# A parameter set for a kernel that orders its own work, and a start whose loads are issued by two engines

## The chip, the cores and the metric

One core of a Trainium2 chip runs the program. The metric is the device time of one execution in microseconds (us). Every time below is of this one core. TensorE is called PE in the views (PEld for its weight loads), VectorE is DVE, ScalarE is ACT, GpSimd is POOL, and SyncE, which issues most transfers, is SP.

## What is computed

For 8 batches, 8 heads, 576 positions and 64 features per head, attention keeps the 32 largest scores of a row, and its result goes through a layer that takes the largest of three products:

```python
scores = scale * np.matmul(q, k.transpose(0, 1, 3, 2))
kth = np.partition(scores, -top_k, axis=-1)[..., -top_k:-top_k + 1]
scores = np.where(scores >= kth, scores, -1000000000.0)
attn = softmax(scores)                       # written out in the reference
x = np.matmul(attn, v).transpose(0, 2, 1, 3).reshape(B * S, H * D)
h = np.maximum(np.maximum(x @ w1, x @ w2), x @ w3)     # 512 -> 768
out = h @ w_out                                        # 768 -> 512
```

q, k and v are float32, the four weights are float64.

## The kernel before

Two heads share one pass (a head pair, 4 pairs to a batch). A unit of work is one pair and 256 of its rows, or two pairs and the last 64 rows of each; a batch has 10 units. A unit goes through these steps. PE computes scores (`qk`, L514), ACT copies them out (`evac`, L523), DVE takes the eight largest of each 72 columns (`sweep`, L532) and finds a pivot (L546 to L563). ACT takes the sign against it (L571), POOL multiplies (L576), DVE takes eight maxima again (L580), picks the 32nd largest and masks (L619). ACT takes the exponential (L628), PE transposes it (`turn`, L674 to L679), ACT copies it out (L687), PE multiplies by v (`values`, L704). DVE, ACT and POOL turn the result into two half-precision parts, `xh` and `xl` (L721 to L728).

The layer (`mlp`) of a batch takes its 576 rows in spans of columns. For a span, each of 6 blocks f of 128 hidden features needs three products of 12 matmuls each (`layer`, L760): 216 matmuls for a span. ACT and DVE keep the largest (L767, L769), ACT and POOL split it into `hh` and `hl` (L772, L775). Then `layer2` (L820) makes 128 output rows with 18 matmuls, ACT scales them (L825) and SP stores them (L831 to L835). Batches 0 to 6 have spans of 256 and 320 columns; `parts_of[B - 1]` (L1056) gives the last batch 256, 256 and 64.

The weights arrive as float64 in 18 blocks (`load_weight`, L229, 768 KB each for the first 12). DVE builds float32 of the two words, half a block at a time (`decode`, L238 to L240): the first half of a block reads the first 768 of its 1536 words in a row. ACT squares the result (L250), PE sums the squares (L259). `load_qk` (L420 to L431) issues the six transfers of one head pair: two for q, two for k, and two for the last 64 rows of k and of q (tile `last`). PE transposes `last`, k and q (L454, L465), ACT and POOL make `kT` and `qT` of them (L469 to L474).

No scheduler of the compiler orders this work. Each step is a `Piece` with an engine, a cost in ns, the pieces it needs, the buffers it takes and a rank. `in_order` (L65) plays the pieces through its own model of the five engines and emits them in that order; each engine then runs its own list strictly in order. A piece's rank is the place of its unit plus a number from the table `OFFSETS`. Of the pieces near the lowest rank (`LEAD`, `WINDOW`), an engine takes the first that can start within `PATIENCE` of the earliest. The layer's pieces are a second list (`fill`), which PE takes where it would otherwise wait (`AHEAD_OF_FILL`). `LOCK_A` and `LOCK_B` say how DVE pieces that read two tensors from SBUF and POOL pieces are kept apart. These constants alone decide which engine does what in which order; the arithmetic does not depend on them.

Of the kernel before, what the change touches and what calls it, by code (L numbers as in the profile page):

```python
# [12 lines left out]
I32 = mybir.dt.int32  # L13
# [15 lines left out]
GAP = 100.0  # L29
NEAR = 110.0  # L30
SWITCH = 95.0
AHEAD_OF_FILL = 3
WINDOW = 150
LEAD = 43.3
SLACK = 2000.0
LOCK_A = -150.0
LOCK_B = -100.0
OFFSETS = {'C0': -8.46, 'C1': -18.47, 'C2': 3.93, 'C3': 15.97, 'D0': -3.87, 'D1': -3.6, 'D2': -21.98, 'D3': 12.25, 'E00': 3.88, 'E01': 0.84, 'E02': -2.21, 'E10': -0.98, 'E11': -2.42, 'E12': -13.91, 'N': 0.27, 'Pa': -3.56, 'Pl': -8.36, 'Pp': 14.6, 'Pz': 7.25, 'R': 10.23, 'S': -1.09, 'T00': -15.17, 'T01': -13.99, 'T02': 4.17, 'T10': -11.04, 'T11': -8.12, 'T12': 22.63, 'U': -1.67, 'U0': 2.18, 'V': -13.7, 'V0': -0.21, 'Y': 0.84, 'Z': -6.48, 'd0': 7.84, 'd1': -2.02, 'e00': -1.82, 'e01': -1.45, 'e10': -1.05, 'e11': 1.55, 'g0': 1.61, 'g1': -2.4, 'g2': 1.3, 'g3': -10.18, 'h0': 2.46, 'h1': -2.33, 'h2': 1.34, 'k0': 0.45, 'k1': -2.6, 'k2': 2.19, 'k3': -8.03, 'm0': -18.11, 'm1': -7.69, 'm2': -3.59, 'm3': -1.01, 'p1': 3.73, 'p2': 4.11, 'p3': -13.92, 'p4': -15.96, 'p5': 2.73, 'q0': -0.76, 'q1': -0.22, 'r0': 1.77, 'r1': -17.21, 's00': 5.74, 's01': 5.23, 's10': 5.37, 's11': 6.45, 'v': 13.6, 'w0': 9.7, 'w1': 11.03, 'w2': 0.57, 'w3': 18.45, 'x0': 3.87, 'x1': 2.76, 'x2': 8.01, 'x3': 5.15, 'y': -13.4, 'z0': 3.01, 'z1': 4.39}
AHEAD = 4
LATE = {'PE': 102.0, 'DVE': 60.0, 'ACT': 95.0, 'POOL': 10.0, 'SP': 2000.0}  # L40

# [91 lines left out]
SPLIT = (0,)  # L133
FIRST = ((0, 1),)
NSM = 2
PATIENCE = {'PE': 2.0, 'DVE': 159.0, 'ACT': 47.0, 'POOL': 7.0, 'SP': 0.0}


@with_exitstack
def kernel(ctx, tc, q, k, v, moe_w1, moe_w2, moe_w3, moe_w_out, out):  # L140
    nc = tc.nc
    B, H, S, D = q.shape
    P = 128
# [76 lines left out]
    def load_weight(j):  # L220
        src, c, n, at0 = parts[j]
        if c % 2 == 0:
            raw = wall.bitcast(I32)[:, 2 * CUT + at0:2 * CUT + at0 + 2 * n]
        elif j < 3 * KC:
            spare = N_IN + 2 * CUT + c // 2 * 2 * DF
            raw = wall.bitcast(I32)[:, spare:spare + 2 * n]
        else:
            raw = wk.tile([P, 2 * n], I32, name="ssb", bufs=NSSB)
        nc.sync.dma_start(raw, src[c * P:(c + 1) * P, :].bitcast(I32))  # L229
        raw_of[j] = raw.rearrange("p (n t) -> p n t", t=2)  # L230

    def decode(j, j0):
# [97 lines left out]
    def weights():  # L330

        decoded, loads, scales = {}, {}, {}
        for i in range(4):
            mine = range(i * KC, (i + 1) * KC) if i < 3 else range(3 * KC, len(parts))
            rank = (0.0, f"D{i}")
            done = []
            release = []
            for j in mine:
                n = parts[j][2]

                free, c = [], parts[j][1]
                takes = [("ssb" if i == 3 else "odd", free)] if c % 2 else []
                needs = [decoded[j - AHEAD]] if j >= AHEAD else []
                if i == 3:
                    needs += [decoded[k] for k in range(3 * KC) if k % 2]
                loads[j] = piece("SP", 5000 if i < 3 else 3400, lambda j=j: load_weight(j), needs, (0.0, f"D{i}"), takes)
                for j0 in range(0, n, PIECE[n]):
                    rel = []
                    x = piece("DVE", 1600 if i < 3 else 1950, lambda j=j, j0=j0: decode(j, j0),
                              [loads[j], *([decoded[j - 1]] if j else []), *([x] if j0 else [])], rank, [("ob", rel), ("ob", rel)], alone=True)  # L350
                    rel.append(x)
                decoded[j] = x
                free.append(x)
                rel = []
                y = piece("ACT", 733 if i < 3 else 510, lambda j=j: square_w(j), [x], rank, [("junk", rel)])
                if i < 3:
                    z = piece("PE", 400, lambda j=j: sum_w(j), [y, *done[-1:]], rank, [("m", release)] * 2 if j % KC == 0 else [])
                    z.slack = SLACK / 4
                    rel.append(z)
                    done.append(z)  # L360
                else:
                    rel.append(y)
                    done.append(y)
            if i < 3:
                scaled = piece("DVE", 1750 if i < 2 else 3000, lambda i=i: column_scale(i), done, rank)
# [27 lines left out]
    def main_rows(t, b, h):  # L393
        return t[at.get(b, b), h, 0:MAIN].rearrange("(p c) d -> p c d", c=NU)
# [24 lines left out]

    def load_qk(b, hp):  # L420
        tiles = []
        for src, nm in ((q, "qt"), (k, "kt")):
            t = io.tile([P, NU, 2, D], F32, name=nm, bufs=1)
            for h in range(2):
                nc.sync.dma_start(t[:, :, h, :], main_rows(src, b, 2 * hp + h))
            tiles.append(t)
        t = io.tile([P, 2, D], F32, name="last", bufs=1)
        for w, src in enumerate((k, q)):
            nc.sync.dma_start(t[64 * w:64 * w + 64], src[at.get(b, b), 2 * hp:2 * hp + 2, MAIN:S].rearrange("h p d -> p h d"))
        tiles.append(t)  # L430
        qk_of[b, hp] = tiles  # L431

# [302 lines left out]
    def mlp(b, first, spans, tiles, alone, needs, rank):  # L735
# [41 lines left out]
        for c0, c1 in spans:  # L777
# [3 lines left out]
            for f in range(FC):  # L781
                box, prev, before = {}, None, []
                for i in range(3):
                    rel = []
                    for kcs in ((0, 1), (2, 3)):
                        x = add("PE", 6 * max(0.423 * w, 64.0), lambda i=i, f=f, kcs=kcs, c0=c0, c1=c1, box=box: layer(i, f, kcs, c0, c1, box),
                                [*needs, *(lows[i * KC + kc, f * P // CUT * CUT] for kc in kcs if lows)],
                                [("m", rel)] if kcs[0] == 0 else [])
                    now = []
                    y = add("DVE" if i else "ACT", 117 + 1.047 * w if i else 152 + 0.844 * w, lambda i=i, w=w, box=box: largest(i, w, box),  # L790
                            [x, *prev] if i else [x], [("h1", now)])
                    rel.append(y)
                    if i:
                        before.append(y)
                    before, prev = now, [y]
# [88 lines left out]
    def attention(n):  # L884
# [3 lines left out]
        half = us[0] == NU  # L888
        gs = range(len(us))
        d = of[n] = {}  # L890
        p = lambda key, *a, **kw: d.setdefault(key, piece(*a, rank=(place_of[n], key if isinstance(key, str) else "".join(map(str, key))), **kw))
# [105 lines left out]

    def prepare(pi):
        b, hp = preps[pi]
        rank = starts[pi]  # L1000
        load = piece("SP", 4000, lambda: load_qk(b, hp), list(load_last), (rank, "Pl"))
        box = {}
        load_last.clear()
        done, last = [], list(load_bits)
# [1 line left out]
        for k in range(3):  # L1006
# [5 lines left out]
            x = piece("PE", 109 if k == 0 else 436, products, [load, *done[-1:]], (rank, "Pp"), [("tr", rel)])  # L1012
            y = piece("ACT", 169 if k == 0 else 1211, lambda k=k: box["turns"][k][1](), [x, *last, *done[-1:]], (rank, "Pa"))
            rel.append(y)
            load_last.append(x)
            if pi >= 2:
                users[pi - 2].append(x)
            done.append(y)
            if k:
                z = piece("POOL", 1380, lambda k=k: box["turns"][k][2](), [y], (rank, "Pz"))  # L1020
                done.append(z)
                load_bits.append(z)
        prepared[pi] = done
# [127 lines left out]
```

## Time and profile before

| what | value |
| --- | --- |
| median of 3 runs | 1278.31 us (1277.34 to 1278.84) |
| the profiled execution | 1279.52 us, span 1277.8 us |
| mean granted clock of TensorE | 0.961 |
| PE busy | 1165.9 us (91%) |
| DVE busy | 1157.3 us (91%) |
| ACT busy | 1118.2 us (88%) |
| POOL busy | 684.9 us (54%) |
| moved by DMA | 53.58 MB, mean 42 GB/s |

The span runs from the first to the last instruction; the execution's own time is 1.7 us longer. Busy shares are averages over stages: at the start DVE and the transfers work and PE has little to do, at the end PE works alone. So the table says little by itself, and the prediction reads the views by stretch of time.

### The profile page before, as it was taken

The page shows a single profiled execution, that of the slowest core. Times are in us where ns is not written, and L with a number is a line of the kernel's source. Part 1 is how long each engine was busy: PE and PEld are TensorE (multiplying, and loading weights), DVE is VectorE, ACT ScalarE, POOL GpSimd, SP SyncE. Part 2 cuts the span into 40 slices and gives each one's busy share as a digit, 9 for nine tenths or more (in the row PEclk, how much of TensorE's full clock was granted, in tenths as well). Part 3 has the DMA queues.
Part 4 walks back from the last instruction along what each step waited for, and adds up shares of the span by engine and source line. Part 5 has one row for each costly group of instructions (what it writes and reads, how often), then busy time and mean ns, then how long its engine had stood idle before and what let it go on. Part 6 is the DMA issues. An engine that isn't in the chain of part 4 may idle for free.

```text
span 1277.8 us, 30699 instructions
## 1 busy us (share of the span) xinstructions
PE 1165.9 (91%) x9949; PEld 855.3 (67%) x9949; DVE 1157.3 (91%) x5736; ACT 1118.2 (88%) x2912; POOL 684.9 (54%) x625
## 2 busy tenths in 40 slices
PE   4337897999799999999999999999999999999997
PEld 3224574766487766867686766867787777867775
DVE  6999999999999999999999999999999999999221
ACT  5699989999999999999999999999999999998321
POOL 4538477664565565655465565555556555545110
PEclk9667899899799999999999999999999999999999
DMA  7341110211011012110111011010111100000000
GB/s 223 129 117 45 51 38 17 49 38 46 20 39 41 25 29 54 30 36 25 51 38 37 20 37 47 20 53 22 46 30 46 30 21 26 20 18 2 17 18 28
DMA packets 107018, 53.58 MB, mean 42 GB/s; under 512 B 91745, under 2 KB 99937, under 8 KB 106849
## 3 DMA queue, kind: packets, MB, share of 16 engines
q1 hardware_dynamic: 106848, 51.54, 14.7%
q8 instruction: 80, 1.31, 0.4%
q14 instruction: 90, 0.73, 0.2%
HBM read 42.07 MB, written 9.44 MB: 40 GB/s over the span
## 4 chain that ended last, share of the span: by engine, by line
PE 33%; DVE 26%; ACT 20%; POOL 4%; issue 2%; SPq 0%; DMA 0%; ACTq 0%; DVEq 0%; POOLq 0%
PE m L760 16%; DVE L L532 6%; DVE ssb L619 6%; DVE Q L580 4%; ACT w L571 4%; PE m L820 4%; ACT pm L628 4%; PE tr L704 4%; ACT pT L687 4%; PE tr L679 4%; POOL w L576 3%; PE s L514 3%; ACT ssb L523 3%; DVE h L769 2%; DVE nR L556 1%
## 5 line engine op out<-in xcount | busy, mean ns | idle before, releaser
L576 POOL TENSOR_TENSOR w<-ssb,w 128x576 f32<-128x576 f32 x288 | 413.6, 1454 | 135.2 <-ACT w L571 134.3
L760 PE MATMUL m<-xh,wall 128*128 128x256 f16 (+2 forms) x2448 | 436.9, 279 | 1.3 <-DVE h L769 0.6
L760 PEld LDWEIGHTS <-wall 128*128 128x128 f16 x3672 | 343.8, 98 | 79.7 <-issue 7.4
L760 PE MATMUL m<-xl,wall 128*128 128x256 f16 (+2 forms) x1224 | 335.2, 279 | 0.0
L532 DVE MAX8 L<-ssb 128x8 f32<-128x72 f32 x2304 | 329.7, 219 | 2.2 <-ACT ssb L523 2.2
L619 DVE SCALAR_TENSOR_TENSOR ssb<-ssb,kth 128x576 f32<-128x576 f32 x288 | 240.8, 864 | 2.3
L628 ACT ACTIVATE pm<-ssb,nb 128x576 f32<-128x576 f32 x288 | 225.5, 785 | 18.5 <-DVE ssb L619 18.3
L571 ACT ACTIVATE w<-ssb,Q 128x576 f32<-128x576 f32 x288 | 226.1, 786 | 6.8 <-DVE Q L563 6.8
L687 ACT COPY pT<-tr 128x512 f32<-128x512 f32 (+1 forms) x432 | 217.8, 520 | 11.3 <-PE tr L676 7.9
L580 DVE MAX8 Q<-w 128x8 f32<-128x576 f32 x288 | 213.9, 750 | 9.7 <-POOL w L576 8.3
L679 PE MATMUL tr<-ident,pm 128*128 128x128 f32 x1152 | 183.3, 285 | 28.4 <-ACT pm L628 13.2
L514 PE MATMUL s<-kT,qT 64*128 64x288 f32 x1920 | 179.8, 322 | 23.0 <-ACT ssb L523 14.7
L523 ACT COPY ssb<-s 128x576 f32<-128x576 f32 x288 | 185.0, 646 | 4.2 <-PE s L514 3.8
L679 PEld LDWEIGHTS tr<-ident,pm 128*128 128x128 f32 x1152 | 130.8, 143 | 80.2 <-ACT pm L628 27.3
L704 PE MATMUL tr<-pT,vt 128*64 128x256 f32 (+1 forms) x1920 | 180.9, 340 | 2.3 <-ACT pT L687 2.1
L514 PEld LDWEIGHTS s<-kT,qT 64*128 64x128 f32 x1920 | 140.6, 195 | 62.0 <-issue 23.8
L775 POOL TENSOR_TENSOR hl<-h,hh 128x256 f16<-128x256 f32 (+2 forms) x102 | 78.3, 768 | 180.2 <-ACT hh L772 171.1
L769 DVE SCALAR_TENSOR_TENSOR h<-m,rises,h 128x256 f32<-128x256 f32 (+2 forms) x204 | 100.4, 492 | 60.1 <-PE m L760 55.9
L704 PEld LDWEIGHTS tr<-pT,vt 128*64 128x64 f32 x1920 | 109.5, 141 | 60.9 <-issue 15.8
L820 PE MATMUL m<-wall,hh 128*128 128x512 f16 x432 | 128.9, 379 | 3.6 <-POOL wall L305 1.9
L728 POOL TENSOR_TENSOR xl<-xs,xh 128x256 f16<-128x256 f32 (+1 forms) x80 | 52.4, 655 | 126.6 <-ACT xh L724 126.6
L474 POOL TENSOR_TENSOR kT<-raws,kT 128x576 fp32r<-128x576 f32 x34 | 49.7, 1462 | 86.2 <-ACT kT L470 83.8
(109 smaller groups left out, 1468.2 us busy)
## 6 DMA issues: line engine op xcount, KB each, us to landing
wall<-in_moe_w_dram SPq DMA_DIRECT2D x12, 768.0 KB, 5.9
qt<-in_q_dram SPq DMA_DIRECT2D x68, 128.0 KB, 2.9
kt<-in_k_dram SPq DMA_DIRECT2D x68, 128.0 KB, 3.0
out_dram<-ob SPq DMA_DIRECT2D x32, 256.0 KB, 2.3
vt<-in_v_dram SPq DMA_DIRECT2D x32, 128.0 KB, 2.1
vt<-in_v_dram SPq DMA_DIRECT2D x32, 64.0 KB, 2.2
vt<-in_v_dram SPq DMA_DIRECT2D x96, 16.0 KB, 2.0
vt<-in_v_dram SPq DMA_DIRECT2D x32, 48.0 KB, 2.2
```

The lines of the kernel that those rows point to most:

```text
L514: nc.tensor.matmul(s[:, h, :HALF], qT[sl, qa, c0:c0 + P], kT[sl, ka, i * HALF:(i + 1) * HALF], start=(n_ == 0), stop=(n_ == len(runs) - 1))
L523: nc.scalar.copy(d["both", g][:, :, i * HALF:(i + 1) * HALF], d["s"].pop((g, i))[:, :, :HALF])
L532: nc.vector.max(d["L"][:, t, k, :], d["ssb"][t][:, k * GW:(k + 1) * GW])
L571: nc.scalar.activation(d["w"][t], d["ssb"][t], AF.Sign, bias=d["Q"][:, t, 0:1], scale=-1.0, accum_out=d["cnt"][:, t:t + 1])
L576: nc.gpsimd.tensor_tensor(d["w"][t], d["ssb"][t], d["w"][t], ALU.mult)
L580: nc.vector.max(d["Q"][:, t, 1:NW], d["w"].pop(t))
L619: nc.vector.scalar_tensor_tensor(ss, ss, d["kth"][:, t:t + 1], ss, ALU.is_lt, ALU.subtract, accum_out=d["lost"][:, t:t + 1])
L628: nc.scalar.activation(d["pm", t // 2][:, t % 2], d["ssb"][t], AF.Exp, bias=d["nb"][:, t:t + 1], scale=-1.0 / SHRINK, accum_out=d["sums"][ ...
L679: nc.tensor.transpose(pt[:, j * P:(j + 1) * P], pm[:, i, 64 * i + j * P:64 * i + (j + 1) * P], ident)
L687: nc.scalar.copy(pT[:, 512 * i:512 * i + m] if i < 2 else pT[:, 8 * P:10 * P], pt[:, :m])
L704: nc.tensor.matmul(to, vt[:, block if i < 4 else 8 + h, :], keys, start=(i == 0), stop=(i == 4))
L760: nc.tensor.matmul(box["ps", i][:, :c1 - c0], a, bb[:, kc, c0:c1], start=(kc == 0 and k == 0), stop=(kc == KC - 1 and k == 2))
```

## The change

Three things are altered in the text.

First, for the first head pair alone, `load_qk` has k and both parts of `last` issued by ACT in place of SP, and the first weight block is loaded in two halves of 768 words; with the costs that the planner has for the first loads, the first block comes second on SP.

Second, the last batch's layer has the spans of all other batches, 256 and 320 columns.

Third, the planner's constants are others: `OFFSETS` has keys of its own for batch 0 (with an underscore ahead), and `LEAD`, `PATIENCE`, `AHEAD_OF_FILL`, `LOCK_A`, `LOCK_B` and one cost are changed.

```diff
-AHEAD_OF_FILL = 3
+AHEAD_OF_FILL = 6
-LEAD = 43.3
+LEAD = 103.6
-LOCK_A = -150.0
-LOCK_B = -100.0
-OFFSETS = {'C0': -8.46, 'C1': -18.47, 'C2': 3.93,
+LOCK_A = -144.0
+LOCK_B = -103.0
+OFFSETS = {'C0': -11.16, 'C1': -38.66, 'C2': 8.85,
...
-PATIENCE = {'PE': 2.0, 'DVE': 159.0, 'ACT': 47.0, 'POOL': 7.0, 'SP': 0.0}
+PATIENCE = {'PE': 87.0, 'DVE': 178.0, 'ACT': 43.0, 'POOL': 73.0, 'SP': 0.0}
...
-        nc.sync.dma_start(raw, src[c * P:(c + 1) * P, :].bitcast(I32))
+        for j0 in range(0, 2 * n, n if j == 0 else 2 * n):
+            m = n if j == 0 else 2 * n
+            nc.sync.dma_start(raw[:, j0:j0 + m], src[c * P:(c + 1) * P, :].bitcast(I32)[:, j0:j0 + m])
...
-                loads[j] = piece("SP", 5000 if i < 3 else 3400, lambda j=j: load_weight(j), needs, (0.0, f"D{i}"), takes)
+                loads[j] = piece("SP", (5000 if j else 3700) if i < 3 else 3400, lambda j=j: load_weight(j), needs, (0.0, f"D{i}"), takes)
...
+        other = nc.sync if qk_of or T_of else nc.scalar
...
-                nc.sync.dma_start(t[:, :, h, :], main_rows(src, b, 2 * hp + h))
+                (other if src is k else nc.sync).dma_start(t[:, :, h, :], main_rows(src, b, 2 * hp + h))
...
-            nc.sync.dma_start(t[64 * w:64 * w + 64], src[at.get(b, b), 2 * hp:2 * hp + 2, MAIN:S].rearrange("h p d -> p h d"))
+            other.dma_start(t[64 * w:64 * w + 64], src[at.get(b, b), 2 * hp:2 * hp + 2, MAIN:S].rearrange("h p d -> p h d"))
...
-                        x = add("PE", 6 * max(0.423 * w, 64.0), lambda i=i, f=f, kcs=kcs, c0=c0, c1=c1, box=box: layer(i, f, kcs, c0, c1, box),
+                        x = add("PE", 6 * max(0.423 * w + 0.9, 29.0), lambda i=i, f=f, kcs=kcs, c0=c0, c1=c1, box=box: layer(i, f, kcs, c0, c1, box),
...
-        rank = starts[pi]
-        load = piece("SP", 4000, lambda: load_qk(b, hp), list(load_last), (rank, "Pl"))
+        rank, first_ = starts[pi], "" if b else "_"
+        load = piece("SP", 4000 if pi else 2400, lambda: load_qk(b, hp), list(load_last), (rank, first_ + "Pl"))
...
-    parts_of[B - 1] = [(True, [(0, 2 * P)], (0, 1)), (False, [(2 * P, 4 * P)], (2, 3)), (False, [(4 * P, S)], (NU,))]
```

Two places show the new order. In the lists, the names ahead of an arrow are tiles that are written; the changed file's line numbers are 2 higher in the weight load and 3 higher from `load_qk` on.

The start of SP before, where `wall` is the weights' tile:

```order
L425 DMA qt<-in_q_dram 128x4x64 x2
L425 DMA kt<-in_k_dram 128x4x64 x2
L429 DMA last<-in_k_dram 64x2x64
L429 DMA last<-in_q_dram 64x2x64
L229 DMA wall<-in_moe_w_dram 128x1536 x2
```

The start of SP in the changed kernel:

```order
L428 DMA qt<-in_q_dram 128x4x64 x2
L231 DMA wall<-in_moe_w_dram 128x768 x2
L231 DMA wall<-in_moe_w_dram 128x1536
L428 DMA qt<-in_q_dram 128x4x64 x2
L428 DMA kt<-in_k_dram 128x4x64 x2
```

The start of ACT in the changed kernel:

```order
L428 DMA kt<-in_k_dram 128x4x64 x2
L432 DMA last<-in_k_dram 64x2x64
L432 DMA last<-in_q_dram 64x2x64
L463 ACT_TABLE_LOAD
L463 ACTIVATE raws<-tr 128x2x64
```

The four transfers of k and `last` moved from SP to ACT, ahead of its table load, and the first weight block stands behind q alone.

PE around the last pair of value products of the main program, before (`tr<-pT,vt` is the value product of one head pair, `m<-wall,hh` belongs to `layer2`):

```order
L820 LDWEIGHTS hl
L820 MATMUL m<-wall,hl 128x512
L704 MATMUL tr<-pT,vt_89 64x64 x10
L704 MATMUL tr<-pT,vt_90 64x64 x10
L820 LDWEIGHTS hh
L820 MATMUL m<-wall,hh 128x512
```

The same place in the changed kernel:

```order
L763 LDWEIGHTS wall
L763 MATMUL m<-xl,wall 128x256
L707 MATMUL tr<-pT,vt_89 64x64 x10
L707 MATMUL tr<-pT,vt_90 64x64 x10
L763 LDWEIGHTS wall
L763 MATMUL m<-xh,wall 128x256
```

Before, PE was still in `layer2` of batch 6 when the last attention products came; now it has finished that and is in the first span of batch 7.

## Rows read from the trace of the kernel before

**Rows 1.** Busy time by stretch: us, then per engine busy us (instructions), clock, DMA share, GB/s

```profile
10.00:128.00 118.00, 58.30 (x310) 37.99 (x310) 113.04 (x437) 92.79 (x225) 67.71 (x64) 0.71 0.40 123
128.00:256.00 128.00, 110.52 (x930) 80.46 (x930) 122.98 (x584) 117.69 (x315) 80.19 (x77) 0.95 0.15 40
...
512.00:640.00 128.00, 127.90 (x1112) 95.11 (x1110) 125.43 (x673) 123.46 (x323) 70.83 (x60) 1.00 0.14 35
...
896.00:1024.00 128.00, 127.79 (x1128) 95.15 (x1127) 124.09 (x648) 124.90 (x329) 74.45 (x63) 1.00 0.15 38
```

**Rows 2.** Chain that ended last, from 1150 us on: start us, us, what

```profile
1190.59 1.32 PE tr L704 x40
1191.90 3.34 PE m L820 x15
...
1196.66 22.27 PE m L760 x204
1218.93 7.77 PE m L820 x36
1226.71 23.58 PE m L760 x216
...
1266.99 4.00 PE m L820 x18
```

**Rows 3.** The same chain, a stretch of batch 6's 320-column span

```profile
1168.24 3.26 PE m L760 x24
```

**Rows 4.** Instructions in order of time, PE, first and last rows of the 64-column span

```profile
1257.89 0.22 PE L760 MATMUL m<-xh,wall 128*128 128x64 f16 x2
...
1266.93 0.59 PE L820 MATMUL m<-wall,hh 128*128 128x512 f16 x2
```

**Rows 5.** Instructions in order of time, all engines, the first 22 us

```profile
0.74 1.28 ACT L460 ACT_TABLE_LOAD   x1 [0.74 <-PEq L1135]
0.74 1.38 SPq L425 DMA_DIRECT2D qt<-in_q_dram  x2
...
2.16 1.30 SPq L425 DMA_DIRECT2D kt<-in_k_dram  x2
...
3.51 0.64 SPq L429 DMA_DIRECT2D last<-in_k_dram  x1
4.19 0.61 SPq L429 DMA_DIRECT2D last<-in_q_dram  x1
4.85 1.07 SPq L229 DMA_DIRECT2D wall<-in_moe_w_dram  x2
...
7.00 0.44 PE L454 MATMUL tr<-ident,last 128*128 128x128 f32 x1 [7.00 <-DMA last<-in_q_dram]
...
7.48 0.28 ACT L460 ACTIVATE raws<-tr 128x128 f32<-128x128 f32 x1 [5.46 <-PE tr L454]
...
9.63 0.36 DVE L238 TENSOR_SCALAR ob<-wall 128x384 int32<-128x384 int32 x1 [8.15 <-DMA wall<-in_moe_w_dram]
...
17.62 4.40 DVE L532 MAX8 L<-ssb 128x8 f32<-128x72 f32 x32
```

**Rows 6.** Busy time by stretch, one us at the start (columns of rows 1)

```profile
2.00:3.00 1.00, 0.00 (x0) 0.00 (x0) 0.00 (x0) 0.02 (x1) 0.81 (x6) 1.00 0.55 126
...
4.00:5.00 1.00, 0.00 (x0) 0.00 (x0) 0.00 (x0) 0.00 (x0) 0.00 (x0) 1.00 0.97 220
```

**Rows 7.** Who waited for whom, DVE, 10 to 1150 us: total us, times, longest

```profile
DVE Q L580 <- POOL w L576: 8.3, 18, 0.9
DVE xs L721 <- PE tr L704: 3.0, 4, 1.8
```

**Rows 8.** Groups of DVE in the first 256 us: busy us, mean ns

```profile
L619 DVE SCALAR_TENSOR_TENSOR ssb<-ssb,kth 128x576 f32<-128x576 f32 x43 | 40.5, 962 | 0.3
...
L239 DVE SCALAR_TENSOR_TENSOR ob<-wall,ob 128x384 int32<-128x384 int32 x24 | 18.1, 754 | 0.8
L240 DVE SCALAR_TENSOR_TENSOR wall<-wall,ob 128x384 int32<-128x384 int32 x24 | 17.1, 714 | 0.8
```

**Rows 9.** One line's instructions: ns min/median/max, L619 to 256 us, L240 to 130

```profile
L619 DVE SCALAR_TENSOR_TENSOR ssb<-ssb,kth x43: 793/814/1949, 63.5 to 253.9; 128x576 f32<-128x576 f32 x43
...
L240 DVE SCALAR_TENSOR_TENSOR wall<-wall,ob x25: 557/559/1641, 11.7 to 117.9; 128x384 int32<-128x384 int32 x24, 128x512 int32<-128x512 int32 x1
```

More of the change, by code (lines that the diff above doesn't have):

```diff
@@ L31 @@
 SWITCH = 95.0
-AHEAD_OF_FILL = 3
+AHEAD_OF_FILL = 6
 WINDOW = 150
-LEAD = 43.3
+LEAD = 103.6
 SLACK = 2000.0
-LOCK_A = -150.0
-LOCK_B = -100.0
-OFFSETS = {'C0': -8.46, 'C1': -18.47, 'C2': 3.93, 'C3': 15.97, 'D0': -3.87, 'D1': -3.6, 'D2': -21.98, 'D3': 12.25, 'E00': 3.88, 'E01': 0.84, 'E02': -2.21, 'E10': -0.98, 'E11': -2.42, 'E12': -13.91, 'N': 0.27, 'Pa': -3.56, 'Pl': -8.36, 'Pp': 14.6, 'Pz': 7.25, 'R': 10.23, 'S': -1.09, 'T00': -15.17, 'T01': -13.99, 'T02': 4.17, 'T10': -11.04, 'T11': -8.12, 'T12': 22.63, 'U': -1.67, 'U0': 2.18, 'V': -13.7, 'V0': -0.21, 'Y': 0.84, 'Z': -6.48, 'd0': 7.84, 'd1': -2.02, 'e00': -1.82, 'e01': -1.45, 'e10': -1.05, 'e11': 1.55, 'g0': 1.61, 'g1': -2.4, 'g2': 1.3, 'g3': -10.18, 'h0': 2.46, 'h1': -2.33, 'h2': 1.34, 'k0': 0.45, 'k1': -2.6, 'k2': 2.19, 'k3': -8.03, 'm0': -18.11, 'm1': -7.69, 'm2': -3.59, 'm3': -1.01, 'p1': 3.73, 'p2': 4.11, 'p3': -13.92, 'p4': -15.96, 'p5': 2.73, 'q0': -0.76, 'q1': -0.22, 'r0': 1.77, 'r1': -17.21, 's00': 5.74, 's01': 5.23, 's10': 5.37, 's11': 6.45, 'v': 13.6, 'w0': 9.7, 'w1': 11.03, 'w2': 0.57, 'w3': 18.45, 'x0': 3.87, 'x1': 2.76, 'x2': 8.01, 'x3': 5.15, 'y': -13.4, 'z0': 3.01, 'z1': 4.39}
+LOCK_A = -144.0
@@ new lines @@
+LOCK_B = -103.0
+OFFSETS = {'C0': -11.16, 'C1': -38.66, 'C2': 8.85, 'C3': 15.4, 'D0': -9.99, 'D1': -8.22, 'D2': -81.18, 'D3': 12.51, 'E00': 4.08, 'E01': -2.19, 'E02': -3.0, 'E10': -1.33, 'E11': -0.86, 'E12': -0.76, 'N': 2.46, 'Pa': -2.78, 'Pl': -3.28, 'Pp': 12.36, 'Pz': 8.29, 'R': 11.36, 'S': -1.3, 'T00': -26.26, 'T01': -16.18, 'T02': 4.68, 'T10': -21.75, 'T11': -0.4, 'T12': 10.44, 'U': -2.04, 'U0': 1.43, 'V': -18.91, 'V0': -4.73, 'Y': -4.58, 'Z': -60.24, '_E00': 2.75, '_E01': -0.61, '_E02': -1.04, '_E10': -13.28, '_E11': 3.84, '_E12': -26.77, '_N': 3.57, '_Pa': -2.51, '_Pl': -12.84, '_Pp': 5.76, '_Pz': 2.38, '_T00': -5.91, '_T01': 7.37, '_T02': 7.73, '_T10': -0.3, '_T11': 4.59, '_T12': 27.39, '_Y': -1.2, '_Z': 8.62, '_d0': 6.3, '_d1': -2.07, '_e00': -5.83, '_e01': -25.22, '_e10': -2.1, '_e11': 1.02, '_g0': -16.34, '_g1': -3.43, '_g2': 2.64, '_g3': -3.02, '_h0': 2.79, '_h1': -0.17, '_h2': -5.37, '_k0': 4.48, '_k1': -8.78, '_k2': 1.54, '_k3': 3.68, '_m0': -32.38, '_m1': -17.41, '_m2': -9.0, '_m3': 3.27, '_p1': -6.95, '_p2': 2.32, '_p3': -22.4, '_p4': -27.41, '_p5': 6.38, '_q0': -5.17, '_q1': -4.87, '_r0': 3.45, '_r1': -10.97, '_s00': 5.22, '_s01': 3.11, '_s10': 4.7, '_s11': 5.75, '_v': 23.47, '_w0': 7.63, '_w1': 6.97, '_w2': 1.71, '_w3': 13.98, '_x0': -0.42, '_x1': 3.54, '_x2': 7.21, '_x3': 7.63, '_y': -21.64, '_z0': -18.26, '_z1': 5.41, 'd0': 11.4, 'd1': -9.42, 'e00': -2.99, 'e01': 1.19, 'e10': -1.73, 'e11': 1.63, 'g0': 3.72, 'g1': -0.38, 'g2': 1.26, 'g3': -7.35, 'h0': 6.11, 'h1': 2.69, 'h2': 5.9, 'k0': -12.61, 'k1': 1.01, 'k2': 6.16, 'k3': -5.02, 'm0': -20.5, 'm1': -9.07, 'm2': -5.94, 'm3': -1.81, 'p1': 6.3, 'p2': 4.76, 'p3': -11.35, 'p4': -14.51, 'p5': 5.46, 'q0': -3.13, 'q1': -3.11, 'r0': 2.08, 'r1': -10.72, 's00': 7.09, 's01': 5.08, 's10': 5.7, 's11': 6.85, 'v': 8.96, 'w0': -10.6, 'w1': 29.31, 'w2': 13.81, 'w3': 24.36, 'x0': 6.61, 'x1': -7.07, 'x2': 13.29, 'x3': 4.76, 'y': -13.75, 'z0': 3.45, 'z1': 0.91}
@@ L890, in attention @@
         d = of[n] = {}
-        p = lambda key, *a, **kw: d.setdefault(key, piece(*a, rank=(place_of[n], key if isinstance(key, str) else "".join(map(str, key))), **kw))
+        p = lambda key, *a, **kw: d.setdefault(key, piece(*a, rank=(place_of[n], ("_" if b == 0 else "") + (key if isinstance(key, str) else "".join(map(str, key)))), **kw))
         needs, takes = [z for k in prep_of[n] for z in prepared[k]], []
@@ L1011, in prepare @@
             rel = []
-            x = piece("PE", 109 if k == 0 else 436, products, [load, *done[-1:]], (rank, "Pp"), [("tr", rel)])
-            y = piece("ACT", 169 if k == 0 else 1211, lambda k=k: box["turns"][k][1](), [x, *last, *done[-1:]], (rank, "Pa"))
+            x = piece("PE", 109 if k == 0 else 436, products, [load, *done[-1:]], (rank, first_ + "Pp"), [("tr", rel)])
+            y = piece("ACT", 169 if k == 0 else 1211, lambda k=k: box["turns"][k][1](), [x, *last, *done[-1:]], (rank, first_ + "Pa"))
             rel.append(y)
@@ L1019, in prepare @@
             if k:
-                z = piece("POOL", 1380, lambda k=k: box["turns"][k][2](), [y], (rank, "Pz"))
+                z = piece("POOL", 1380, lambda k=k: box["turns"][k][2](), [y], (rank, first_ + "Pz"))
                 done.append(z)
```

## The prediction

> **What bounds the kernel now.** I read the busy time by stretch first, because the averages over the span mix three regimes. From 10 to 128 us DVE is busy 113.0 of 118 us while PE is busy 58.3 at a mean clock of 0.71: DVE sets the pace and PE waits for it. From 128 to 256 us that still holds (DVE 123.0 of 128, PE 110.5). From 512 us on both are full: PE 127.9 of 128 us, DVE 125.4 [rows 1]. The list of waits confirms that DVE loses little to others: between 10 and 1150 us its largest total is 8.3 us for POOL, in 18 waits, and the next is 3.0 us for PE [rows 7]. The chain that ended last shows the third regime. From the end of the last value products, 1191.90 us, it is PE's own work almost without a break to the end of the last `layer2` at 1266.99 + 4.00 = 1270.99 us: 79.1 us in which attention is over and only the layer's products are left [rows 2]. The reader should see there that a product removed from this tail, or done before it, shortens the run one for one, since nothing else is going on beside it.
>
> So the time is: when DVE starts, plus how long the two full engines take for attention, plus what the layer has left when attention ends. The change touches all three.
>
> **The start.** Before, SP issues q, k and `last` in a row and comes to the first weight block at 4.85 us; the block is there when DVE begins to decode it at 9.63 us, 4.8 us after its issue. DVE has waited 8.15 us for it [rows 5]. In the changed order that block stands behind q alone, so SP reaches it at about 2.16 us, where k's issue began: 2.69 us earlier. Were its landing as slow as the whole block's, DVE would start at 2.16 + 4.8 = 6.9 us, 2.7 us sooner. DVE's first decode needs only the first half. A half can land no sooner after its issue than the much smaller `last`, which took from 4.19 to 7.00 us, 2.8 us; that gives 5.0 us and a gain of 4.7, the far end. PE's first transposition waits for `last` [rows 5]. ACT now issues k (1.30 us) and `last` (0.64 and 0.61): the second part is issued at about 0.74 + 1.30 + 0.64 = 2.7 us in place of 4.19, so PE, and behind it ACT and POOL, start up to 1.5 us sooner. ACT pays these four issues and then its table load of 1.28 us, ready at about 4.6 us; its first real work began at 7.48 us after an idle time of 5.46 us, so this is covered, at no cost [rows 5]. No row shows how long ACT takes for an issue. If twice SP's time, `last` is issued at 4.6 us, 0.4 us late, and the table load ends at 7.1: a loss of at most 0.5 us on that path. DVE's path carries the term, because DVE decodes for 8 us (9.63 to 17.62) before its first maxima and is the busy engine from there [rows 1, 5]. I take 2.5 us of gain, near the row of the whole block, with 4.7 and -0.5 as ends. The other moves at the start (a square one place earlier, sums of squares between score products) fall into ACT and PE time that the first stretch has in plenty [rows 1]; were it gone, they are a few us of ACT and PE, which the rivals' price covers.
>
> **The last batch's spans.** Before, the last 64 columns have a span of their own: 216 matmuls from 1257.89 to 1266.93 us, 9.04 us, or 42 ns each, with PE waiting for the short steps of the other engines in between [rows 4]. A span of 256 columns takes 23.58 us for 216, 109.2 ns each [rows 2]. At 320 columns 24 matmuls take 3.26 us, 135.8 ns each [rows 3]. So 216 matmuls of 64 columns go (9.04 us) and 216 become 26.6 ns longer (5.75 us): 3.3 us less. The `layer2` products stay at 54 for these three tiles. This lies in the tail, where nothing covers it, and has one answer.
>
> **What is left at the end.** I counted the layer's matmuls that stand in PE's list ahead of the last pair of value products. Before: 1512 of 256 columns, 1512 of 320, 543 of `layer2`. Changed: 1524, 1512 and 558. That is 12 x 109.2 ns + 15 x 7.77/36 us = 1.3 + 3.2 = 4.5 us of layer work that now comes before the end of attention [rows 2]. If attention ends when it did, the tail is 4.5 us shorter still. If PE was truly full ahead of it, those 4.5 us push the last value products back and nothing is won. From 896 to 1024 us PE is busy 127.8 of 128 us, but DVE, at 124.1, is no less full [rows 1], so I take half, 2.3 us, with 0 and 4.5 as ends. As a check, the changed tail from the rows: 204 matmuls at 22.27 us, 216 at 135.8 ns (29.3 us) and 90 of `layer2` (19.4 us) make 71.0 us in place of 79.1.
>
> The Trainium skill (Perfetto Trace Analysis, Identifying the Most-Contended Engine) says that matmul busy time is a bad measure of how full TensorE is, and that the busy share of weight loads is better. Loads are busy 95.1 of 128 us here. By that rule there is room, the whole 4.5 us would be won and the sum below would come out 2.2 us lower.
>
> **The rest of the order.** The same number of instructions runs on DVE but for 12 short ones less; they are permuted within a batch. The counts at the ends of the batches stay within 10 us of PE work of each other. I price this at zero, and its ends below by the rivals.
>
> **The sum.** 2.5 + 3.3 + 2.3 = 8.1 us less than the profiled execution's 1279.5 us: 1271.4 us. That execution lies 1.2 us above the median of the runs, 1278.3 us, so the forecast for the median is **1270.2 us**; its own range, from the terms' ends, is 1265.8 to 1275.5 (12.5 and 2.8 us of gain). A measurement of this kernel can tell a change of about 0.2%, 2.6 us, from none.
>
> **Rivals.**
>
> *Fewer collisions in batch 0* (gain beyond the forecast). In the first 256 us DVE's instructions that read two tensors are sometimes held: L619 has a mean of 962 ns against a shortest of 793, L239 and L240 means of 754 and 714 against a shortest of 557 [rows 8, 9]. That is 43 x 169 + 24 x 197 + 24 x 157 ns = 15.8 us, on the engine that sets the pace there. The new table places batch 0's pieces apart from the others' by keys of their own. If half of these delays go, 7.9 us more are won: 1262.3 us. For it: the delays are there and the kernel waits for DVE. Against it: most come from POOL running beside DVE, which any order has. Chance 0.15.
>
> *The transfers set the start.* From 4 to 5 us the DMA engines are 97% busy at 220 GB/s, and from 2 to 3 us only 55% [rows 6]. If the first transfers are limited by the engines, k on another queue comes no sooner, and the half block shares what is there: the start gives nothing and the time is 1272.7 us. The Trainium skill (DMA: Bandwidth & Descriptors, Issuing engines are not separate DMA queues) states this: transfers from several engines run on the same 16 DMA engines, and only issue time is saved. The rows at 2 to 3 us speak against it as a full explanation, since the engines were not full while SP was still issuing. Chance 0.13.
>
> *Balance.* The start gives nothing, early layer work pushes attention back by as much, and waits elsewhere return the cut: 1275.7 to 1280.8 us, the same within 0.2%, or just over the edge of faster. Chance 0.11.
>
> *Layer work in the way of attention* (slower). At the end of batch 1 the changed PE list has 366 matmuls of 256 columns ahead of the last value products where there were 276: 90 x 109.2 ns = 9.8 us of layer work earlier. In that stretch DVE is near full and depends on PE's transpositions and scores. If DVE waits for all of it and never catches up, 9.8 - 2.5 - 3.3 = 4.0 us are lost: 1282.3 us. It decides when DVE's waits for PE in the first 400 us grow by more than the 5.8 us won elsewhere. Against it: PE is idle 17.5 of 128 us from 128 to 256 us [rows 1], which takes up such work. Chance 0.11.
>
> **How the numbers follow.** The forecast has 0.50. It, the collisions and the transfers are faster by over 0.2%: 0.50 + 0.15 + 0.13 = 0.78, and 0.01 of the balance makes 0.79. Same has the other 0.10, slower 0.11. The range from 1260.0 to 1278.5 us leaves out about 0.05 below (more collisions gone than half, and a better tail) and 0.15 above (the slower case and the upper part of the balance).
>
> **What would show it.** Right: DVE's first decode starts between 5 and 7.5 us; no matmul of 64 columns at L763; from the last value products to the last `layer2` 71 us in place of 79; the last value products 1 to 4 us earlier than 1190.59. The collisions would show as means of L242 and L622 nearer to their shortest, and last value products 8 us or more earlier. The transfers would show as a first decode no sooner than 9 us. Layer work in the way would show as waits of DVE for PE between 200 and 400 us. The prediction is wrong if the last value products come later than 1190.59 us although DVE started sooner: then the new order costs attention more than the counts in the lists let me see.

## The result, and the profile after

| | before | changed |
|---|---|---|
| median of the runs, us | 1278.05 (1276.21 to 1279.25, 6 runs) | 1266.87 (1266.32 to 1268.97, 6 runs) |
| ratio, 95% interval | | 0.9917 [0.9904, 0.993] |
| profiled execution: own time, span | 1279.52, 1277.8 | 1266.59, 1264.8 |
| end of the last value products | 1191.91 | 1186.76 |
| end of the last `layer2` | 1270.99 | 1258.03 |
| tail between these two | 79.08 | 71.27 |

The change is faster by 0.8%, 11.2 us by the medians; the forecast was 1270.2 us. Lines of the changed kernel stand 2 or 3 higher than before (L707 are the value products that were L704, L763 the layer's products that were L760). First the chain that ended last, from 1180 us on (start us, us, what), against [rows 2, 4]:

```profile
1185.45 1.31 PE tr L707 x40
1186.77 2.73 PE m L763 x24
...
1189.60 19.65 PE m L763 x180
1209.25 7.77 PE m L823 x36
1217.02 29.34 PE m L763 x216
1246.36 11.67 PE m L823 x54
1258.11 0.69 ACT ob L828
```

The 64-column span is gone: 216 products take 29.34 us in one piece where 23.58 and 9.04 stood. Behind the last value products there are no `layer2` products left over from batch 6 (15 before). The tail is 7.8 us shorter. The other 5.1 us of the 13.0 between the two spans come from attention, which ends sooner. At the start (instructions in order of time, the first 22 us), against [rows 5]:

```profile
0.74 1.35 ACTq L428 DMA_DIRECT2D kt<-in_k_dram  x2
...
2.40 1.78 SPq L231 DMA_DIRECT2D wall<-in_moe_w_dram  x3
2.80 0.63 ACTq L432 DMA_DIRECT2D last<-in_q_dram  x1
...
7.51 0.36 DVE L240 TENSOR_SCALAR ob<-wall 128x384 int32<-128x384 int32 x1 [6.04 <-DMA wall<-in_moe_w_dram]
...
8.08 0.45 PE L457 MATMUL tr<-ident,last 128*128 128x128 f32 x1 [8.08 <-DMA last<-in_q_dram]
...
15.67 4.61 DVE L535 MAX8 L<-ssb 128x8 f32<-128x72 f32 x32
```

DVE's first decode starts 2.1 us sooner, the first maxima 1.95 us. `last` is issued 1.4 us sooner and lands later all the same: PE's first transposition starts at 8.08 us in place of 7.00. ScalarE's issues take as long as SyncE's (1.35, 0.65 and 0.63 us for what took 1.30, 0.64 and 0.61). The busy time by stretch (columns as in [rows 1]) of the changed kernel:

```profile
10.00:128.00 118.00, 58.36 (x312) 37.41 (x310) 112.64 (x457) 97.81 (x236) 70.36 (x66) 0.65 0.40 123
...
256.00:384.00 128.00, 120.97 (x1063) 90.77 (x1060) 125.18 (x648) 121.58 (x322) 75.09 (x63) 0.97 0.13 33
...
512.00:640.00 128.00, 127.88 (x1121) 95.48 (x1118) 125.37 (x651) 125.24 (x331) 73.79 (x65) 1.00 0.14 37
...
10.00:1152.00 1142.00, 1053.32 (x8940) 771.19 (x8939) 1111.20 (x5608) 1070.84 (x2800) 659.84 (x574) 0.96 0.16 43
```

and two of these stretches before:

```profile
256.00:384.00 128.00, 116.82 (x1003) 85.52 (x1000) 124.28 (x645) 122.07 (x321) 74.46 (x62) 0.95 0.14 35
...
10.00:1152.00 1142.00, 1045.38 (x8860) 765.39 (x8861) 1107.20 (x5557) 1065.19 (x2780) 652.93 (x570) 0.96 0.16 43
```

PE is busy 7.9 us more in the same 1142 us, 4.2 us of it between 256 and 384 us, where it had been idle for 11 of 128 us; DVE is not held up by it; it is busy 4.0 us more as well. The layer's products do not simply move to that place and stay ahead: counted in the traces, 61 more of them than before have started by 384 us, 17 more by 768 us and 39 more by 1186 us. In between the time goes to attention, whose 144th mask of 288 ends at 629.2 us in place of 637.5.

### The profile page after: what moved, and what is told of

Same layout as the page of the kernel before. It is cut to its first block, busy times and chain, and to the rows that moved or that the text cites. A ratio compares the mean times of both kernels' runs of the same rounds, so it can differ in the third digit from the quotient of the medians.

```text
span 1264.8 us, 30228 instructions
## 1 busy us (share of the span) xinstructions
PE 1161.1 (92%) x9733; PEld 846.4 (67%) x9733; DVE 1152.2 (91%) x5724; ACT 1113.4 (88%) x2900; POOL 685.7 (54%) x619
## 4 chain that ended last, share of the span: by engine, by line
PE 58%; DVE 20%; ACT 17%; issue 2%; POOL 2%; DMA 1%; SPq 0%; ACTq 0%; POOLq 0%; DVEq 0%
PE m L763 24%; PE tr L707 8%; PE m L823 8%; PE s L517 8%; PE tr L682 7%; DVE L L535 4%; ACT w L574 4%; DVE ssb L622 4%; ACT pm L631 3%; ACT pT L690 3%; DVE Q L583 3%; ACT ssb L526 2%; PE tr L468 1%; DVE wall L242 1%; DVE ob L241 1%
## 5 line engine op out<-in xcount | busy, mean ns | idle before, releaser
L763 PE MATMUL m<-xh,wall 128*128 128x256 f16 (+1 forms) x2304 | 433.6, 286 | 1.3 <-ACT h L770 0.6
L763 PEld LDWEIGHTS <-wall 128*128 128x128 f16 x3456 | 336.1, 98 | 84.1 <-issue 7.8
L763 PE MATMUL m<-xl,wall 128*128 128x320 f16 (+1 forms) x1152 | 329.2, 286 | 0.0
L622 DVE SCALAR_TENSOR_TENSOR ssb<-ssb,kth 128x576 f32<-128x576 f32 x288 | 237.4, 851 | 2.5
L682 PE MATMUL tr<-ident,pm 128*128 128x128 f32 x1152 | 180.6, 284 | 22.3 <-ACT pm L631 11.0
L707 PE MATMUL tr<-pT,vt 128*64 128x256 f32 (+1 forms) x1920 | 180.2, 339 | 1.2 <-ACT pT L690 1.2
L707 PEld LDWEIGHTS tr<-pT,vt 128*64 128x64 f32 x1920 | 109.0, 140 | 60.6 <-issue 17.1
L778 POOL TENSOR_TENSOR hl<-h,hh 128x256 f16<-128x256 f32 (+1 forms) x96 | 77.5, 808 | 132.4 <-ACT hh L775 132.1
L772 DVE SCALAR_TENSOR_TENSOR h<-m,rises,h 128x256 f32<-128x256 f32 (+1 forms) x192 | 97.3, 507 | 49.7 <-PE m L763 48.4
```

The costliest lines, as they stand in the source:

```text
L622: nc.vector.scalar_tensor_tensor(ss, ss, d["kth"][:, t:t + 1], ss, ALU.is_lt, ALU.subtract, accum_out=d["lost"][:, t:t + 1])
L682: nc.tensor.transpose(pt[:, j * P:(j + 1) * P], pm[:, i, 64 * i + j * P:64 * i + (j + 1) * P], ident)
L707: nc.tensor.matmul(to, vt[:, block if i < 4 else 8 + h, :], keys, start=(i == 0), stop=(i == 4))
L763: nc.tensor.matmul(box["ps", i][:, :c1 - c0], a, bb[:, kc, c0:c1], start=(kc == 0 and k == 0), stop=(kc == KC - 1 and k == 2))
```

## The experiments

The kernel before ran beside every group of runs, with medians of 1277.3 to 1277.9 us, and each ratio below is against it. None of the twelve leaves work out.

**The start undone in the changed kernel.**

```
-        other = nc.sync if qk_of or T_of else nc.scalar
+        other = nc.sync
-        for j0 in range(0, 2 * n, n if j == 0 else 2 * n):
...
+        nc.sync.dma_start(raw, src[c * P:(c + 1) * P, :].bitcast(I32))
```

> The changed kernel, but with the first head pair's k and the last rows issued by SyncE again and the first weight block loaded whole; order table, costs and spans stay as changed. If the start is a term of its own: VectorE's first decode back from 7.5 to about 9.6 us, the tail after the last value products still about 71 us, and the time about 2 us above the changed kernel (1268 to 1270, where the changed one runs at 1266.9). If transfers or the later landing of the last rows set the start anyway: within 1 us of the changed kernel. If the start's gain is spent in batch 0's queueing: first decode 2 us later, time the same.

1269.01 us, ratio 0.9933 [0.9921, 0.9946]: 2.1 us above the changed kernel. The first decode starts at 9.47 us and the tail is 71.26 us. The two intervals overlap, so the medians alone do not settle a term of 2 us; the trace does: DVE's masks (L622) end 1.6 to 2.4 us later than in the changed kernel from the first to the last. The start is a term of its own.

**The 64-column span again, in the changed kernel.** One line, the old `parts_of[B - 1]`, is put back.

> The changed kernel with the last batch's spans 256, 256 and 64 again, all else as changed. If the cut of the 64-column span is worth what its rows say, the tail after the last value products grows by 9.04 - 5.75 = 3.3 us, and the time by as much (about 1270.2). If the planner's other span only moved work from one side of the last value products to the other, the time stays within 1 us.

1271.18 us, 0.9948 [0.9935, 0.9961]: 4.3 us above the changed kernel. The tail is 74.55 us, 3.28 us longer:

```profile
1186.20 1.31 PE tr L707 x40
...
1217.77 23.58 PE m L763 x216
...
1258.06 4.00 PE m L823 x18
```

Attention ended 0.75 us later in this profile; the last 0.3 us of the 4.3 are within the spread of the medians.

**The span alone, and the start alone, in the kernel before.** The first takes that line away, the second makes the edits of `load_weight` and `load_qk` only.

> The kernel before with the last batch in two spans of 256 and 320 columns, and nothing else of the change. Terms that add: 3.3 us under the kernel before (about 1274.8), with the tail after the last value products at 79.1 - 3.3 = 75.8 us. If the spans pay only together with the new order: within 1 us of the kernel before.

> The kernel before with the start alone: k and last rows issued by ScalarE, the first weight block second and in two transfers; order and spans as before. Terms that add: first decode at about 7.5 us in place of 9.6, the time about 2 us under the kernel before (1276). If TensorE's start, which the last rows release, sets the pace of the first batch: no gain, or up to 1 us slower, since these rows land about 1 us later.

The span alone: 1276.38 us, 0.9987 [0.9978, 0.9996]. The tail is 75.82 us, the 3.26 us shorter that the rows give:

```profile
1187.92 1.31 PE tr L704 x40
...
1224.04 29.34 PE m L760 x216
1253.38 11.67 PE m L820 x54
```

But the median is only 1.4 us lower. In all its runs the time stands 2.1 to 2.2 us above the span of the core, in the kernel before 1.7 to 1.8, which takes 0.4 of the missing 1.9 us; the rest stays open. The start alone: 1276.81 us, 0.9992 [0.9984, 1.0001], 0.9 us lower where 2 was expected, and not told apart from no change, although the first decode starts at 7.20 us. So both parts are there in the trace, and something outside them gives or takes some 2 us.

**The new order alone,** the planner's constants, offsets and costs with the old start and spans.

```
-LEAD = 43.3
+LEAD = 103.6
...
-PATIENCE = {'PE': 2.0, 'DVE': 159.0, 'ACT': 47.0, 'POOL': 7.0, 'SP': 0.0}
+PATIENCE = {'PE': 87.0, 'DVE': 178.0, 'ACT': 43.0, 'POOL': 73.0, 'SP': 0.0}
```

> The kernel before with the new order alone: the planner's constants, offsets and costs of the changed kernel, batch 0's own keys among them; the start and the last batch's three spans as before. Terms that add: the changed kernel plus the start (2.1, measured with the start undone) plus the span (3.2 us longer tail in the run with 64 columns), so 1272 to 1274, with a tail after the last value products of about 74.5 us in place of 79.1. If TensorE is full and the layer work done ahead only pushes attention back: the tail as short, the last value products as much later, and the time within 2 us of the kernel before. If the order pays only with the new start: 1276 or more.

1273.34 us, 0.9968 [0.9956, 0.998]: 4.0 us faster than the kernel before, and in the expected 1272 to 1274. Its chain shows the tail, with 15 `layer2` products fewer and the 64 columns still there:

```profile
1185.98 1.32 PE tr L705 x40
1187.30 2.73 PE m L761 x24
...
1252.54 5.30 PE m L761 x132
1257.84 4.00 PE m L821 x18
```

1261.84 - 1187.30 = 74.54 us, 4.54 us less than before. With the 3.26 us of the span this makes 71.28, and the changed kernel has 71.27: the two terms of the tail add to a hundredth of a us. The order gains 4.0 us by the medians and 4.5 us in the tail, so attention as a whole was not pushed back by the layer work put ahead of its end. This is the net of everything that the new constants do; the moved products alone have no run that isolates them. The medians of the single parts do not add up to the change: 1.4 + 0.9 + 4.0 = 6.3 us where it gains 11.2. On top of the new order the spans and the start together gain 6.5 us (1266.87 against 1273.34), on the old order 2.3 by their single runs. What makes this difference was not found.

**Layer products held back.** A test of that last point in the other direction. A table of the changed kernel's own order fixes the sequence of attention's instructions on every engine; the layer's pieces on PE then take the places that stood 7 or 14 pieces later.

```
-            some = [x for x in queues[e][:WINDOW] if x.rank <= low + LEAD]
-            some = some + fills[e][:1] if e == "PE" else fills[e][:1] + some
+            some = queues[e][:1]
+            some = some + (fills[e][:1] if may(len(queues[e]), len(fills[e])) else []) if e == "PE" else fills[e][:1] + some
...
+BEHIND = 7
+def may(left, fills):
+    j = len(STOOD) - fills + BEHIND
+    return 779 - left >= (STOOD[j] if j < len(STOOD) else 779)
```

> The changed kernel with attention's instructions in the same order on every engine, but the layer's products held back on TensorE by 7 pieces (of 6 products, or 3 of the second layer), so that 7 more of them, about 4.5 us, lie behind the last value products. If TensorE has room ahead of the end of attention: last value products within 1 us of the changed kernel's, tail 71.3 + 4.6 = 75.9 us, time 1271.4. If TensorE is full there: last value products 4.5 us sooner, the time as the changed kernel's. If the half that the prediction took is right: 2.3 us slower.

> As the run with 7 pieces held back, with 14 pieces, about 9.1 us. If TensorE has room: last value products unmoved, tail 80.4 us, time about 1276. If it is full: last value products 9 us sooner, the time as the changed kernel's. Half: 4.5 us slower.

> The control for the two runs that hold the layer's products back: the same table that fixes the order of attention's instructions, with 0 pieces held back. If the 50 and 68 us come from where the layer's products stand: within 2 us of the changed kernel. If the fixed order itself, or the layer's short steps that the planner places anew on the other engines, cost them: 1280 or more.

None of the three theories holds for the first two: 1317.18 us (ratio 1.0306 [1.0291, 1.0321]) and 1335.13 us (1.0446 [1.0431, 1.046]). The tails are as reckoned, 75.81 and 81.15 us (75.9 and 80.4 were expected). But attention itself takes longer, little by little over the whole span: with 7 pieces the 144th of the 288 masks (L622) ends 15 us later than in the changed kernel, the last one 45 us. The busy time by stretch of that run shows PE and DVE both less full than in the rows above:

```profile
256.00:384.00 128.00, 120.18 (x1010) 85.83 (x1007) 120.47 (x621) 116.86 (x307) 69.29 (x59) 0.96 0.12 31
...
512.00:640.00 128.00, 124.14 (x1075) 92.47 (x1075) 123.84 (x644) 122.10 (x320) 69.63 (x62) 1.00 0.13 31
```

The control with nothing held back runs in 1273.29 us, 0.9965 [0.9952, 0.9978]. Its masks end within 0.8 us of the changed kernel's up to the 144th; the last one ends 3.6 us later. The control also has some of the layer's short steps in other places on DVE, ACT and POOL (from 369 us on, the first L772 on DVE); that these cost the 3.6 us was not shown. So some 44 of the 50 us come from where the layer's products stand between attention's instructions. Whether that is PE's own places or those of the layer's steps on ACT, DVE and POOL that follow them was not taken apart.

**Batch 0 placed by the other batches' offsets.**

```
-        p = lambda key, *a, **kw: ... ("_" if b == 0 else "") + (key if ...
+        p = lambda key, *a, **kw: ... (key if ...
-        rank, first_ = starts[pi], "" if b else "_"
+        rank, first_ = starts[pi], ""
```

> The changed kernel with batch 0 placed by the offsets of the other batches instead of keys of its own; the spans, the start and the costs as changed, so the tail stays at about 71 us. If the separate keys bring the fewer held instructions in the first 256 us: means of the mask and decode lines back to those of before (962, 754, 714 ns) and 3 us or more lost by 256 us. If they are only one of many orders of equal worth: within 3 us of the changed kernel. If, as with the products held back, any shift of the layer's products against attention costs much: 10 us or more, lost gradually over the span.

1304.65 us, 1.0215 [1.0202, 1.0228]: 37.8 us slower than the changed kernel. The held instructions do not explain it: the mask line's mean is 948 ns to 256 us, between the 936 and 963 of runs with the changed order. The tail is 69.3 us. The loss is not gradual: from 10 to 128 us DVE is busy for 96.56 us in place of 112.64, at the 18th mask it is 44 us late, later 12 to 44, and 40 at the last. So this order needs the keys of its own for batch 0.

**The start in its parts.** The changed kernel with the two transfers alone (the first line below), with ScalarE's issues alone (the second), and with `last` issued ahead of k (the rest).

```
+        other = nc.sync
...
+        nc.sync.dma_start(raw, src[c * P:(c + 1) * P, :].bitcast(I32))
...
+        if first:
+            rows(first[0])
         for src, nm in ((q, "qt"), (k, "kt")):
```

> The changed kernel with k and the last rows issued by SyncE again, the first weight block still in two transfers. If the place of the issue sets VectorE's start: the first decode comes 2 us later, at about 9.5 us less what a half lands sooner than the whole, and the time is that of the run with the start undone (1269). If the size of the transfer sets it: first decode near 7.5 us and the time near 1267.

> The changed kernel with the first weight block in one transfer again; k and the last rows still issued by ScalarE, the block second. If the early issue brings most of the start: first decode at 7.5 to 8.5 us and a time of 1267 to 1268.5. If the two transfers are needed for it: first decode at 9 us or later and the time that of the run with the start undone, 1269. If neither transfer decides and the first 360 us settle by chance within some 2 us, as the run with halves alone (first decode 8.38, 1271.2) suggests: a time that does not follow the first decode, between 1266 and 1271.

> The changed kernel with ScalarE issuing the last rows before k instead of after it. In the changed kernel TensorE's first transposition waits for these rows until 8.08 us, 1.1 us longer than before. If that delay costs time: first transposition at 7 us or sooner and the time about 1 us lower (1266). If VectorE sets the pace of the first batch: first transposition sooner, or held by k instead, and the time within 0.5 us of 1266.9.

| | first decode | PE's first | median, us | ratio |
|---|---|---|---|---|
| start undone | 9.47 | 6.71 | 1269.01 | 0.9933 [0.9921, 0.9946] |
| two transfers alone | 8.38 | 6.97 | 1271.20 | 0.9948 [0.9934, 0.9962] |
| ScalarE's issues alone | 8.44 | 8.73 | 1269.20 | 0.9923 [0.991, 0.9936] |
| the change | 7.51 | 8.08 | 1266.87 | 0.9917 [0.9904, 0.993] |
| `last` ahead of k | 6.29 | 4.94 | 1268.88 | 0.9933 [0.992, 0.9947] |

Each part brings the first decode forward by about 1 us, and together they bring 2. The times do not follow: the earliest decode of all is 2.0 us slower than the change by the medians, a difference that their overlapping intervals do not settle. The traces, one of each kernel, show where these two part. Up to 115 us the DVE of the run with `last` ahead is only 0.2 us behind the changed kernel; from the 13th to the 16th mask it falls 2.6 us behind, and it stays 2.2 to 2.9 us behind nearly to the end. PE in order of time from 117 us, in the changed kernel:

```profile
116.75 0.66 PE L468 MATMUL tr<-ident,qt 128*128 128x128 f32 x4 [0.55 <-ACT pT L690]
...
119.77 0.66 PE L517 MATMUL s<-kT,qT 64*128 64x288 f32 x6 [2.15 <-ACT ssb L526]
120.62 0.95 PE L517 MATMUL s<-kT,qT 64*128 64x288 f32 x6 [0.18 <-ACT ssb L526]
121.50 3.70 PE L707 MATMUL tr<-pT,vt 128*64 128x256 f32 x20
```

and with `last` ahead of k, where all lines stand 4 higher:

```profile
116.89 1.12 PE L472 MATMUL tr<-ident,qt 128*128 128x128 f32 x4 [0.55 <-ACT pT L694]
...
120.59 1.93 PE L521 MATMUL s<-kT,qT 64*128 64x288 f32 x12 [2.15 <-ACT ssb L530]
122.45 4.53 PE L711 MATMUL tr<-pT,vt 128*64 128x256 f32 x20
```

The same four transpositions take 0.66 and 1.12 us. DVE, in order of time in the second run, then waits for these value products, which it does not do in the changed kernel:

```profile
127.03 0.48 DVE L728 SCALAR_TENSOR_TENSOR xs<-tr,down_v,pT 128x256 f32<-128x256 f32 x1 [1.16 <-PE tr L711]
```

That wait is 1.16 us of the 2.6. The rest is DVE's own masks, which take longer around it; in the changed kernel:

```profile
123.30 0.80 DVE L622 SCALAR_TENSOR_TENSOR ssb<-ssb,kth 128x576 f32<-128x576 f32 x1
...
127.97 1.28 DVE L622 SCALAR_TENSOR_TENSOR ssb<-ssb,kth 128x576 f32<-128x576 f32 x1
```

and with `last` ahead:

```profile
123.38 1.40 DVE L626 SCALAR_TENSOR_TENSOR ssb<-ssb,kth 128x576 f32<-128x576 f32 x1
...
130.05 1.91 DVE L626 SCALAR_TENSOR_TENSOR ssb<-ssb,kth 128x576 f32<-128x576 f32 x1
```

The busy time by stretch shows PE's part of it in the granted clock (third number from the end): first the changed kernel, then the run with `last` ahead.

```profile
115.00:120.00 5.00, 2.07 (x15) 1.49 (x16) 5.00 (x29) 5.00 (x15) 4.32 (x4) 1.00 0.19 43
120.00:125.00 5.00, 4.82 (x32) 2.76 (x30) 4.90 (x26) 4.97 (x14) 3.40 (x3) 0.66 0.34 76
```

```profile
115.00:120.00 5.00, 2.66 (x14) 1.76 (x12) 5.00 (x29) 4.41 (x13) 4.45 (x4) 0.68 0.10 24
120.00:125.00 5.00, 4.41 (x24) 2.96 (x26) 4.90 (x21) 4.97 (x14) 2.54 (x3) 0.50 0.43 96
```

A clock of 1.00 is TensorE's upper level, 2.4 GHz, and 0.50 the lower, 1.2 GHz. From 90 to 110 us PE is busy for 11 of 20 us and its clock is at 0.50 in both. In the changed kernel it is back up for all of 115 to 120 us, in the other run not. A low clock in these two stretches is not enough for the wait. The run with the 64-column span has it too:

```profile
115.00:120.00 5.00, 4.02 (x16) 2.86 (x16) 4.98 (x29) 4.08 (x12) 4.25 (x5) 0.50 0.01 2
120.00:125.00 5.00, 3.44 (x20) 2.48 (x22) 4.90 (x19) 4.97 (x13) 2.55 (x3) 0.50 0.52 118
125.00:130.00 5.00, 3.54 (x26) 1.99 (x22) 5.00 (x19) 5.00 (x16) 4.61 (x4) 0.98 0.54 188
```

but there the clock rises while the 20 value products run, they take 3.25 us in place of 4.53, and DVE does not wait for PE. The control with nothing held back shows the same (0.50 and 0.58, 3.20 us, no wait). The run with the two transfers alone shows the wait twice: 0.73 and 0.50 in these two stretches with 1.1 us of waiting, and 0.86 from 330 to 350 us (1.00 in the changed kernel) with this wait:

```profile
336.55 0.48 DVE L724 SCALAR_TENSOR_TENSOR xs<-tr,down_v,pT 128x256 f32<-128x256 f32 x1 [1.50 <-PE tr L707]
```

At this second place the traces agree: from 330 to 340 us the clock is 0.71 here and 0.75 with ScalarE's issues alone, where DVE waits 1.8 us for the same products; in the six other runs with this order and nothing held back (the changed kernel, the start undone, the 64-column span, the order alone, `last` ahead and the control) it is 0.91 to 1.00 and DVE does not wait for PE.

## Why the prediction was right, and where it was off

The direction and the range held, and each of the three terms is in the traces; their sum was 3 us short. Two of the signs fell just outside what was written: the first decode starts at 7.51 us, and the last value products come 5.1 us earlier in the profiles, not 1 to 4. By their own steps:

- **The start** was put at 2.5 us, with a first decode near 6.9. It came at 7.51, 2.1 us sooner, and undoing the start costs 2.1 us. The issue moved by 4.85 - 2.40 = 2.45 us where 2.69 was reckoned. What was not foreseen is that a half then takes 5.1 us to land, longer than the whole block's 4.8 [rows 5]: from 5 to 8 us the DMA engines are full (busy shares 1.02, 1.04 and 1.07). In the same stretch the step "PE starts up to 1.5 us sooner" failed: it started 1.1 us later, although `last` was issued 1.4 us sooner. No run shows a cost of this: with `last` ahead of k PE starts at 4.94 us, and DVE's first twelve masks end no sooner than in the changed kernel. The Trainium skill (DMA: Bandwidth & Descriptors, Issuing engines are not separate DMA queues) says that issuing on several engines saves only the time to issue; the traces agree: with ScalarE's issues alone the whole block is issued 2.44 us sooner than with the start undone, and the first decode starts 1.03 us sooner, less than that.
- **The last batch's spans** were put at 3.3 us. The tails differ by 3.26 and 3.28 us in the two pairs of kernels that differ in this alone.
- **Layer work ahead of the end** is the term that was mis-sized. The count of 4.5 us was exact (79.08 against 74.54), but the prediction took half of it, because "from 896 to 1024 us PE is busy 127.8 of 128 us, but DVE, at 124.1, is no less full". By the medians of the order alone, 4.0 us with an interval from 2.6 to 5.6, the half is too little and all of it can have been won. One stretch near the end was the wrong row to ask: PE's busy time grows by 7.9 us over the whole span, 4.2 us of it between 256 and 384 us, where it was idle for 11 us. That this idle time is what took the work in is an account of busy times; no run tested it, as the ones made for it lost far more. The weight-load rule that the prediction weighed (the Trainium skill, Perfetto Trace Analysis, Identifying the Most-Contended Engine), and from which it took that all of the 4.5 us would be won, gave the right sum; but no run here shows that it did so for its reason.
- **The rest of the order at zero** came out right for this table, by luck more than by its reason. Order alone gains 4.0 us where its tail gains 4.5. But 7 pieces held back cost 44 us beyond the control, and batch 0 with the common offsets 38: the step "they are permuted within a batch, I price this at zero" has no general ground, and the slower rival, priced at 4.0 us, priced far too low what a bad placement can do.

With the whole 4.5 us and the measured start the sum is 2.1 + 3.3 + 4.5 = 9.9 us, against 11.2 by the medians. The remaining 1.3 us are within the interval of the ratio (9 to 12 us); where they come from was not shown. The profiled execution of before lay 1.5 us above its median, which accounts for most of the difference to the 13.0 between the spans.

Of the rivals, *fewer collisions* does not hold: the mask line's mean is 936 ns in the changed kernel's profile, but 963 in that of ScalarE's issues alone and of the control, whose batch 0 runs in all but the same order; 936 and 963 are 1.2 us over 44 masks. The two decode lines go from 754 and 714 ns to 699 and 696, 1.8 us over 24 of each, where the rival needed 7.9 us. *The transfers set the start* is half right: they set how late a half lands, not whether DVE starts sooner. *Balance* and *layer work in the way* are out: DVE waits for PE in none of its rows between 200 and 400 us in the changed kernel (1.8 us before).

## What to carry to other kernels

A tail that follows one engine can be counted: products taken out of it or put ahead of its start add up to a hundredth of a microsecond in the tail. Whether they come free is not read from one full stretch near the end; idle time of the engine in any stretch ahead may pay for them. An order that was tuned as a whole must be judged as a whole: moving one stream a few places against another cost 44 us here, ten times what the moved work itself takes. A gain of 2 us at the start can be made or lost again a hundred microseconds later, so measure such a part by undoing it, several times, and look in the trace for the place where two runs part. Gains measured one at a time need not add: here they came to 6.3 us of 11.2.

## What the runs showed that was not expected

TensorE's clock can decide a single wait of DVE, although PE is not the engine that sets the pace there. With PE busy about half of the time up to 150 us, the clock moves between 0.50 and 1.00, at moments that differ from one kernel to the next although the work is the same. In the changed order, where it stays low while the value products at 122 to 127 us or those at 330 to 340 us run, DVE waits 1.1 to 1.8 us for them. With `last` ahead of k this wait is 1.16 us, about half of the 2.3 us by which its attention ends later in the trace; the longer masks beside it are the rest, and why they are longer was not taken apart. The two transfers alone fall behind by 2.6 us at the first place and 1.6 us at the second, make up some of it in between, and end attention 4.2 us late. No run changed the clock by itself, and each kernel left one trace, so that the clock also sets the differences of the medians is likely but not shown. The same holds for the 1.5 us missing from the span alone.
